# First batch of a retention and Fourier-mixing kernel: k transposed from f32, DFT sums and residual kept in PSUM, a new order

## The chip, the cores and the metric

The kernel runs on one core of a Trainium2 chip. The metric is the device time of one execution in microseconds, the median of several runs. The engines are PE (matrix products), DVE (vector), ACT (activations and copies), POOL (general) and SP, which here only starts transfers. They run side by side, each in its own order, and wait for one another through semaphores.

## The reference

Two stages follow each other. The first is linear attention with decay, for 4 batches, 8 heads, 768 positions and 64 columns per head:

```
state = gamma[h] * state + outer(k[t], v[t])
y[t]  = (1/8) * q[t] @ state
```

The heads side by side give x, 768 x 512 per batch. The second stage mixes by a Fourier transform and applies an MLP:

```
mixed = real(fft over columns (fft over positions (x)))
u     = x + mixed
un    = (u - mean(u)) / sqrt(var(u) + 1e-6)
out   = u + relu(un @ w_ch1) @ w_ch2        # 512 -> 2048 -> 512
```

Both weights and all inputs are f32 in memory; the output is 4 x 768 x 512 f32.

## The kernel before

**Attention.** Heads are treated in pairs, in the order 0, 1, 3, 2, and positions in 6 chunks of 128. For each pair q, k and v are loaded as f32 (`load_unit`, line 159), three transfers of 384 KB. POOL casts q (`q0_unit`, line 392), casts k with the decay of its position in the chunk (`k0_unit`, lines 401 to 408) and casts v (`v0_unit`, line 417), all to f16. PE transposes q and the cast k (`t0_unit`, line 433) into PSUM, six blocks each, and ACT copies them out as qT and kT (`te_unit`, lines 441 and 444). Within a chunk, PE forms scores (`am_unit`, line 458) and DVE multiplies them by a causal mask and a constant that takes the decay of k back (`ae_unit`, line 465, four instructions of 384 columns per pair). Across chunks, PE forms the products of k and v (`kv0_unit`, line 480) and DVE runs one scan over the chunks (`sc_unit`, line 489). Two groups of products, from the masked scores (`yi_unit`, line 504) and from the states (`yx_unit`, line 520), add up in PSUM, and ACT writes them, scaled, into x (`x0_unit`, line 533). x is kept in two sides: heads 0 to 3 in order, heads 4 to 7 mirrored.

**Fourier mixing.** The real transform is done by symmetry. DVE forms sums and differences of the two halves of the positions (`fold_s`, line 673), then sums and differences of the two mirrored sides (`fold_d`, line 683). PE multiplies them by cosine and sine tables over positions (`s1_unit`, line 730; four groups, each twice three products of 193 columns). ACT and DVE copy the four results into g (lines 737 and 739). Column 0 is treated apart (`g0_unit`), with a cosine table csn. The second transform (`s2_unit`, lines 843 and 847) uses tables over columns; its cosine part and sine part stand next to each other in PSUM, and their sum gives columns 0 to 256, their difference, read backwards, the rest. ACT copies the sine part to SBUF (qn, line 855) and DVE adds both, with column 0, into u (lines 856 and 858). For the first three row blocks of the first batch half of x has been added to both parts in PSUM before (`px_unit`, line 797). The mean of a row of u comes from a row sum of x (`xmean_unit`, line 711) and column 0 (`mean_unit`). The other three row blocks use g mirrored (`gr_unit`).

**MLP.** ACT writes un = mean - u (line 879), PE transposes it (`unT_unit`, line 914), ACT and DVE copy it out (lines 916 to 921). The first layer of the first three row blocks is done block by block (`h0_unit`, line 947: a row block and a quarter of the 2048 columns per unit, 16 products), all others in widths of 384 (`h_unit`, line 930). ACT and DVE evict with a relu. The second layer (`ch_unit`, line 973) gathers 16 products of 512 columns in one bank; DVE scales by the inverse deviation, adds u (line 977), and SP stores.

**Order.** The first batch is a written list (`first_units`): each unit is emitted in turn, and `pin` chains every instruction behind the one before it on its engine, so the list is the order on all engines. Where PE has nothing to do, `filler` puts products of zeros (line 145) into a bank of their own. Weights are loaded by POOL (lines 987 and 994) in eight transfers. After the first batch, the units of all batches carry due times on a scale of batches (`emit`), and a scheduler orders each engine; the next batch's loads wait for the seventh weight transfer and for one h0 product. The setup computes the sine and cosine tables on DVE and ACT (`trig_dve`, `t_act`) among the attention units.

PSUM has eight banks: five for the pool "g", two for "y" and one for the fillers; after the first batch, three of them become the MLP's pool "pm".

Of the kernel before, what the change touches and what calls it, by code (L numbers as in the profile page):

```python
# [32 lines left out]
NPE = 2  # L33
ACT_ROWS = ((2, 5, 6, 7, 8, 9, 10, 14), (0, 3, 6, 7, 9, 10, 11, 12, 14, 15), (2, 4, 5, 6, 7, 8, 10, 14))
# [3 lines left out]
def kernel(  # L38
# [32 lines left out]
    first = ExitStack()  # L71
    ps_y = first.enter_context(tc.tile_pool(name="ps_y", bufs=2, space=PSUM))
    ps_w = first.enter_context(tc.tile_pool(name="ps_w", bufs=1, space=PSUM))
    ps_pm = None
# [65 lines left out]
    wps = ps_w.tile([P, DM], f32, tag="w", name="wps")  # L140

    def filler(n):
        def run():
            for _ in range(n):
                nc.tensor.matmul(wps, wz[:, 0:P], wz, start=True, stop=True)  # L145
        return run
# [5 lines left out]
    def load_unit(b, i, after=None):  # L152
        def run():
            h0 = 2 * PAIR_ORDER[i]
            for name, src in srcs.items():
# [3 lines left out]
                dma = nc.sync.dma_start(t, src[b, h0:h0 + 2].rearrange(rows, p=P))  # L159
# [21 lines left out]
    gexp = const.tile([P, 2, H], f32, tag="gexp")  # L181
    gq8, gkd = gexp[:, 0], gexp[:, 1]
    ident16 = const.tile([P, P], f16, tag="ident16")
    tmp = up.tile([P, NCH, DM], f32, tag="u32", name="tmp")
# [3 lines left out]
    rs = [tmp[:, 2 + n] if n < 4 else tmp2[:, n - 4] for n in range(10)]  # L188
    icoln = const.tile([P, 5], f32, tag="icoln")
# [8 lines left out]
    for h in range(H):  # L198
# [6 lines left out]
                            op0=ALU.mult)  # L205
    nc.scalar.activation(gexp, gexp, AF.Exp, bias=0.0, scale=1.0)
# [4 lines left out]
    make_identity(nc, ident16)  # L211
    nc.gpsimd.affine_select(out=maskf, in_=maskf, compare_op=ALU.is_ge, fill=0.0, base=0,
# [15 lines left out]

    def late_consts():
        with tc.issue_after(lb[0]["una"].ins):  # L230
            for h in range(H):
                nc.scalar.activation(maskp[:, h // 2, h % 2], maskf, AF.Copy, bias=0.0,
                                     scale=float(gam[h] ** (-P)))
# [59 lines left out]
    def csn_unit(c):  # L293
        def run():
            nc.scalar.activation(csn[:, c, :], rs[2 * c + 1][:, 0:384], AF.Sin, bias=hpi,
                                 scale=-float(2.0 * np.pi / S))
        return run
# [46 lines left out]
    def half_ids():  # L344
        nc.gpsimd.tensor_scalar(out=hid, in0=ident16, scalar1=0.5, scalar2=1.0, op0=ALU.mult,
                                op1=ALU.mult)
        nc.gpsimd.tensor_scalar(out=nhid, in0=ident16, scalar1=-0.5, scalar2=1.0, op0=ALU.mult,
                                op1=ALU.mult)

# [3 lines left out]
    at, q16_of, kd_of, v16_of, last_cast = {}, {}, {}, {}, {}  # L353
# [42 lines left out]
    def k0_unit(i):  # L396
        def run():
            h0 = 2 * PAIR_ORDER[i]
            k32 = in_of.pop(("k", 0, i))
            kd = kd_of[0, i] = kp.tile([P, NCH, 2, D], f16, tag="kd16", name="kd16")  # L400
            nc.gpsimd.tensor_scalar(out=kd[:, :, 0, :], in0=k32[:, 0], scalar1=gkd[:, h0:h0 + 1],
                                    scalar2=1.0, op0=ALU.mult, op1=ALU.mult)
            if i < 3:
                nc.gpsimd.tensor_scalar(out=kd[:, :, 1, :], in0=k32[:, 1],
                                        scalar1=gkd[:, h0 + 1:h0 + 2], scalar2=1.0,
                                        op0=ALU.mult, op1=ALU.mult)
            else:
                nc.scalar.activation(kd[:, :, 1, :], k32[:, 1], AF.Copy, bias=0.0,
                                     scale=gkd[:, h0 + 1:h0 + 2])
        return run  # L410

    def v0_unit(i):
        def run():
            v32 = in_of.pop(("v", 0, i)).rearrange("p h c d -> p c h d")
            v16 = v16_of[0, i] = vp.tile([P, NCH, 2, D], f16, tag="v16", name="v16")
            n = NCH if i < 3 else 3
            last_cast[0, i] = nc.gpsimd.tensor_scalar(
                out=v16[:, 0:n], in0=v32[:, 0:n], scalar1=1.0, scalar2=1.0, op0=ALU.mult,
                op1=ALU.mult)
            if n < NCH:  # L420
                nc.vector.tensor_copy(v16[:, n:], v32[:, n:])
        return run

    def t0_unit(i, part):
        def run():
            if part == 0:
                at[0, i] = dict(kT=tp.tile([P, NCH, P], f16, tag="kT", name="kT"),
                                qT=qts[i % 2][:, 0])
            src = (q16_of, kd_of)[part][0, i]
            tq = at[0, i]["tq", part] = ps_g.tile([P, NCH, P], f16, tag="g", name="tq",  # L430
                                                  padded_shape=[P, 8, P])
            for c in range(NCH):
                nc.tensor.transpose(tq[:, c, :], src[:, c].rearrange("p a b -> p (a b)"), ident16)
        return run

    def te_unit(i, part):
        def run():
            st = at[0, i]
            tq = st["tq", part]
            if part == 0:  # L440
                nc.scalar.copy(st["qT"].rearrange("p c t -> p (c t)").rearrange(
# [736 lines left out]
```

## Time and profile before

| what | value |
|---|---|
| median of 3 runs | 247.5 us |
| span of the profiled execution | 246.0 us |
| PE, DVE, ACT, POOL busy | 95%, 72%, 51%, 33% |
| fillers (line 145) | 40 products, 13.3 us of PE |
| first product of the MLP (line 947) | at 35.15 us |
| second layer of the first batch (line 973) | from 48.5 us |

A row of a list of groups has the line, the engine, the operation, what it writes from what it reads, the shape and the count; then busy microseconds, the mean in nanoseconds, and the idle time ahead of it with what ended it. A row of the timeline has the start, the length, the engine, the line and the operation; in brackets the wait ahead of it. A row of a table of stretches has the stretch and its length, then the busy time and the number of instructions of each engine, the granted PE clock, the share of the DMA engines and GB/s.

### The profile page before, as it was taken

How to read it: one execution, taken by the hardware profiler on the slowest of the kernel's cores; microseconds unless marked ns; L12 is line 12 of the kernel's file. 1: busy time of each engine (PE TensorE's matmuls, PEld its weight loads, DVE VectorE, ACT ScalarE, POOL GpSimd, SP SyncE). 2: the span in 40 equal slices, each digit the busy share in tenths (PEclk: the TensorE clock that was granted, in tenths of full speed). 3: DMA queues.
4: the chain of work that ended last, by engine and by line, in shares of the span. 5: the costliest groups of instructions: out<-in, count | busy, mean ns of one | idle time of the engine just before them, and what ended most of it. 6: DMA issues, size and time to landing. Idle time of an engine off the chain costs nothing.

```text
span 246.0 us, 5309 instructions
## 1 busy us (share of the span) xinstructions
PE 234.4 (95%) x2024; PEld 144.4 (59%) x2024; DVE 177.5 (72%) x430; ACT 124.3 (51%) x276; POOL 81.3 (33%) x146
## 2 busy tenths in 40 slices
PE   6897899999999999999999999999999998999994
PEld 2454668956676655665567446665666455445543
DVE  8998957898788788995987648887895657424122
ACT  8798669477785445742247415732257217202500
POOL 6667600376500068690001637660003214000000
PEclk9999999999999999999999999999999999999999
DMA  8998999699999287988999589596100331121012
GB/s 174 257 260 138 200 204 206 152 250 261 275 233 214 56 171 176 190 174 149 242 266 210 119 183 181 108 138 150 58 0 3 60 133 30 38 85 43 0 45 85
DMA packets 99209, 36.39 MB, mean 148 GB/s; under 512 B 89840, under 2 KB 96240, under 8 KB 99184
## 3 DMA queue, kind: packets, MB, share of 16 engines
q1 hardware_dynamic: 94960, 31.86, 62.5%
q0 software_dynamic: 4224, 4.19, 10.5%
q8 instruction: 16, 0.26, 0.5%
q14 instruction: 9, 0.07, 0.1%
HBM read 27.26 MB, written 6.29 MB: 136 GB/s over the span
## 4 chain that ended last, share of the span: by engine, by line
PE 72%; DVE 8%; POOL 7%; ACT 4%; SPq 3%; DMA 2%; issue 2%; POOLq 0%; DVEq 0%
PE psc L973 30%; PE psh L930 23%; SPq L159 3%; PE ps L730 3%; PE psh L947 3%; PE wkA L594 3%; DMA k<-in_k_dram 2%; PE wkY L648 2%; POOL u L864 2%; POOL u L866 2%; PE wkY L644 1%; DVE bst L883 1%; PE wkK L613 1%; DVE u L834 1%; PE pq L827 1%
## 5 line engine op out<-in xcount | busy, mean ns | idle before, releaser
L973 PE MATMUL psc<-w,ht 128*128 128x512 f16 (+1 forms) x400 | 89.6, 370 | 0.1
L930 PE MATMUL psh<-unT,w 128*128 128x384 f16 x448 | 81.3, 326 | 0.6 <-ACT ht L934 0.6
L973 PEld LDWEIGHTS <-ht 128*128 128x128 f16 x400 | 38.1, 98 | 35.5 <-issue 0.3
L930 PEld LDWEIGHTS <-w 128*128 128x128 f16 x448 | 42.3, 98 | 24.9 <-issue 1.3
L934 ACT ACTIVATE ht<-psh 128x384 f16<-128x384 f32 x64 | 30.6, 488 | 39.4 <-PE psh L930 38.3
L864 POOL TENSOR_TENSOR u<-u,x 128x256 f32<-128x256 f32 x21 | 13.3, 634 | 102.3 <-DVE u L834 90.7
L977 DVE SCALAR_TENSOR_TENSOR ob<-psc,stats,u 128x512 f32<-128x512 f32 (+1 forms) x25 | 18.1, 722 | 27.4 <-PE psc L973 27.3
L936 DVE TENSOR_SCALAR ht<-psh 128x384 f16<-128x384 f32 x48 | 26.3, 551 | 8.6 <-PE psh L930 8.3
L597 DVE TENSOR_TENSOR atm<-wkA,maskp 128x512 f16<-128x512 f32 x36 | 23.9, 685 | 1.0 <-PE wkA L594 1.0
L885 ACT ACTIVATE un<-u,stats 128x512 f16<-128x512 f32 x21 | 15.1, 721 | 16.9 <-DVE stats L884 8.7
L883 DVE BATCH_NORM_STATS2 bst<-u 128x6 f32<-128x512 f32 x21 | 14.6, 694 | 9.7 <-POOL u L866 9.5
L623 DVE SCALAR_TENSOR_TENSOR s<-s,gk,wkK 128x128 f16<-128x128 f16 x48 | 16.4, 343 | 2.3 <-ACT s L619 1.4
L656 ACT ACTIVATE x<-wkY,gexp 128x384 f16<-128x384 f32 x24 | 12.8, 580 | 9.3 <-PE wkY L648 9.3
L145 PE MATMUL wps<-ht 128*128 128x512 f16 x40 | 13.3, 439 | 2.2 <-POOL ht L196 2.2
L377 POOL TENSOR_SCALAR kd<-k,gexp 128x384 f16<-128x384 f32 x24 | 13.8, 584 | 2.4 <-DMA k<-in_k_dram 2.4
L866 POOL TENSOR_TENSOR u<-u,x 128x256 f32<-128x256 f32 x21 | 13.3, 634 | 2.8 <-DVE u L837 1.5
L594 PE MATMUL wkA<-qTz,kT 128*128 128x256 f16 x72 | 13.6, 273 | 0.0
L829 ACT COPY qn<-pq 128x128 f32<-128x128 f32 x18 | 4.9, 274 | 14.1 <-PE pq L827 13.9
L947 PE MATMUL psh<-unT,w 128*128 128x128 f16 x192 | 11.5, 219 | 0.1
L947 PEld LDWEIGHTS <-w 128*128 128x128 f16 x192 | 11.0, 98 | 0.7 <-issue 0.5
L382 POOL TENSOR_SCALAR v<-v 128x768 f16<-128x768 f32 x12 | 10.0, 830 | 2.0 <-DMA v<-in_v_dram 1.9
L594 PEld LDWEIGHTS <-kT 128*128 128x128 f16 x72 | 6.9, 98 | 6.0 <-DVE s L623 0.4
(164 smaller groups left out, 318.2 us busy)
## 6 DMA issues: line engine op xcount, KB each, us to landing
q<-in_q_dram SPq DMA_DIRECT2D x16, 384.0 KB, 6.2
k<-in_k_dram SPq DMA_DIRECT2D x16, 384.0 KB, 5.6
v<-in_v_dram SPq DMA_DIRECT2D x16, 384.0 KB, 6.6
out_dram<-ob SPq DMA_DIRECT2D x23, 256.0 KB, 2.6
w<-in_moe_w_ch_dram POOLq DMA_DIRECT2D x8, 512.0 KB, 11.1
out_dram<-ob SPq DMA_DIRECT2D x2, 128.0 KB, 1.7
unT<-un SPq DMA_TRANSPOSE x15, 2.4
qTz<-q16z SPq DMA_TRANSPOSE x8, 3.8
```

Source lines behind the costliest of these rows:

```text
L594: mm = nc.tensor.matmul(wk[:, c2], st["kT"][:, c, :], st["qT"][:, :, c, :], start=True, stop=True)
L597: nc.vector.tensor_tensor(out=st["atm"][:, 2 * part:2 * part + 2], in0=wk, in1=maskp[:, PAIR_ORDER[i]].unsqueeze(1).to_broadcast([P, 2, 2, ...
L623: nc.vector.scalar_tensor_tensor(out=s16[:, c], in0=s16[:, c - 1], scalar=gk2[:, hp:hp + 1], in1=wk[:, c - c0], op0=ALU.mult, op1=ALU.add)
L864: nc.gpsimd.tensor_tensor(out=u[:, kb, 0:256], in0=u[:, kb, 0:256], in1=x[:, kb, 0, 1:257], op=ALU.add)
L866: nc.gpsimd.tensor_tensor(out=u[:, kb, 256:512], in0=u[:, kb, 256:512], in1=x[:, kb, 1, 257:1:-1], op=ALU.add)
L883: nc.vector.bn_stats(bst, u[:, kb, :])
L930: nc.tensor.matmul(psh, w116[:, cb, fb * P:(fb + 1) * P], unT[:, cb, rt * 384:(rt + 1) * 384], start=(cb == 0), stop=(cb == 3))
L934: nc.scalar.activation(ht16[:, fb, :], psh, AF.Relu, bias=0.0, scale=-1.0)
L936: nc.vector.tensor_scalar(out=ht16[:, fb, :], in0=psh, scalar1=-1.0, scalar2=0.0, op0=ALU.mult, op1=ALU.max)
L947: mm = nc.tensor.matmul(psh[:, f], w116[:, cb, fb * P:(fb + 1) * P], unT[:, cb, kb * P:(kb + 1) * P], start=(cb == 0), stop=(cb == 3))
L973: nc.tensor.matmul(psc[:, c0:c1], ht16[:, fb, rb3 * P:(rb3 + 1) * P], w216[:, fb, c0:c1], start=(fb == 0), stop=(fb == NFB - 1))
L977: nc.vector.scalar_tensor_tensor(out=ob[:, c0:c1], in0=psc[:, c0:c1], scalar=lb[b]["st"][:, rb, 3:4], in1=lb[b]["u"][:, rb, c0:c1], op0=AL ...
```

## The change

It rewrites the way of the first batch from the loads to the MLP. Its aims, piece by piece:

- k is loaded in halves and transposed on PE straight from f32, so that the transposes need not wait for the cast; the mask's scalar then carries the whole decay (`gks`), different for each row, in place of a constant. Transposes and evictions of k are done in halves of three chunks.
- v is cast by POOL alone. One of the 16 masks is split: ACT scales (`ac_unit`), POOL multiplies by the mask (`am2_unit`).
- `fold_d` is not used for the first batch: both sides are summed by PE, with the sine table once as it is and once negated (`nssp`, made by POOL or ACT), so each group has twice six products. Its eviction becomes a unit of its own (`ge_unit`).
- For row block 0 the residual x and both parts of the second transform are added up in PSUM, in natural order of the columns, with reversed tables (`sr_unit`); un is then written from PSUM directly, one half by ACT and one by DVE (`pn_unit`), and u later (`pu_unit`). Row blocks 1 and 2 keep the old form, in units of their own.
- csn is copied from the position cosines instead of being computed (`csn_unit`).
- The banks are divided into five "g" and three "pm" from the beginning; fillers take turns in "pm" and may be narrower than 512 columns.
- The order is a list of names, `ORDER`. It has far fewer fillers after the first pair, and eight of the twelve h0 units are in it with their evictions; four (blocks 1 and 2, quarters 0 and 2) are left to the due times. The mask constants of later batches (`late_consts`) come later. The weights' quarters are loaded in the order 2, 0, 3, 1 and 1, 2, 0, 3.

The core of the diff:

```diff
+ORDER = """
+f24_90 ts0 q0 ts2 ta02 ta00 tq0 f8_91 tka0 eq0 ts1 tkb0 eka0 f2_4 gk3 f2_10 f1_2 v0 ekb0 ta20
...
+ta30 a20 x10 f1_5 q3 kv2 a21 m200 ta32 ta40 pn2 m210 ta01 tq3 ka3 yi20 m201 x11 w12 sc2 eq3 m211
+ta31 kb3 tka3 tkb3 eka3 fsl yi21 yx2 ekb3 a30 cn0 a31 m300 v3 tL0 ac301 m311 x21 w10 kv3 m310
+x20 sL1 sc3 pm301 ta42 tL1 sr1 ta41 fs0 yx3 w13 yi31 yi30 tR0 vx31 w11 x30 sL0 g0a xm0 fs1 w21
+sR0 xm2 g0b sR1 w22 ae00 g0c ve10 tR1 af01 w20 px0 vf11 s20 w23 mean2 mean0 px2 an00 vn01 xm1
+px1 gr1 ut0 mean1 s21 xe1 au00 vu01 aq1 s22 u0 h00 aq2 u1 h02 gr3 am1 u2 h03 e00 am2 ut1 h01 e02
+vu1 e03 ut2 h13 e01 au2 h11 e13 gr2 h21 e11 h23 e21 gr0 e23
+""".split()
...
+                if b == 0 and name == "k":
...
+                    for h2 in range(2):
+                        dma = nc.sync.dma_start(t[:, :, h2], flat[:, h2])
...
+            for c3 in range(3):
+                nc.tensor.transpose(tk[:, c3, :], k32[:, 3 * half + c3].rearrange(
+                    "p a b -> p (a b)"), ident32)
...
-                scalar=float(gam[2 * PAIR_ORDER[i] + h2] ** (-P)),
+                scalar=gks[:, 2 * PAIR_ORDER[i] + h2:2 * PAIR_ORDER[i] + h2 + 1],
                 in1=maskf.unsqueeze(1).to_broadcast([P, 3, P]), op0=ALU.mult, op1=ALU.mult)
...
+                for n in range(6 if direct else 0):
+                    i0, n = 2 + P * cb, 2 * (n % 3) + n // 3
+                    if part is None or n % 2 == part:
+                        nc.tensor.matmul(ps[:, par, :],
+                                         fd[b]["ab"][:, par, n // 2, n % 2, i0:i0 + P],
+                                         tab[:, par, n // 2, :], start=par == 0 and n == 0,
+                                         stop=n == 5, skip_group_check=True)
...
+            for n in sides:
+                nc.tensor.matmul(pq[n], ident16, xts[0][:, kb, n, slice(257, 1, -1) if n else
+                                                        slice(1, 257)],
+                                 start=True, stop=False, skip_group_check=True)
...
+            else:
+                nc.scalar.activation(dst, pq[n], AF.Identity, bias=fd[0]["mu"][:, kb:kb + 1],
+                                     scale=-1.0)
...
-            for kb in range(3):
-                if kb:
-                    majors.append(unT_unit(0, kb))
-                majors += [h0_unit(kb, g) for g in range(4)]
+            majors += [lambda: None] * 8 + [h0_unit(int(x[0]), int(x[1])) for x in "22 20 12 10".split()]
...
+                streams.append(([late_consts], 0.1, 0.14))
```

In `ORDER`, tq, tka, tkb are transposes of q and of both halves of k, eq, eka, ekb their evictions, a the scores, m the masks, kv and sc the products and the scan, yi and yx the two groups of y, x or vx the evictions by ACT or DVE, fs the folds, sL, sR, tL, tR the products of the first transform (cosine and sine, left and right side), s20 to s22 the second, w the weight transfers, and f with a number the fillers in units of 128 columns.

## The prediction

> **What bounds the kernel now.** I read the page's busy shares first, then three stretches, then the order of time from the last load to the first MLP matmul.
>
> ```profile
> PE 234.4 (95%) x2024; PEld 144.4 (59%) x2024; DVE 177.5 (72%) x430; ACT 124.3 (51%) x276; POOL 81.3 (33%) x146
> ```
>
> PE is the bound on average, but the page mixes a front with fillers and a solid rest. Cut at the first MLP matmul (35.15 us) and at the first matmul of the second MLP layer (48.5 us), PE, PEld, DVE, ACT and POOL were busy for:
>
> ```profile
> 2.15:35.15 33.00, 28.79 (x326) 16.57 (x327) 29.89 (x67) 26.16 (x56) 19.66 (x35) 1.00 1.17 218
> 35.15:48.50 13.35, 13.10 (x212) 12.27 (x212) 9.23 (x23) 9.98 (x28) 2.71 (x8) 1.00 0.96 177
> 48.50:246.00 197.50, 192.48 (x1491) 115.53 (x1488) 137.15 (x328) 86.83 (x192) 57.51 (x94) 1.00 0.66 136
> ```
>
> From 35.15 us PE hardly waits. Before it, 13.31 us of PE's time are the idle-time fillers of line 145:
>
> ```profile
> 0.00:35.15 35.15, 13.31 (x40) 3.72 (x40) 1.00 1.10 206
> ```
>
> So only the moment matters at which the MLP of the first batch starts; each microsecond won there should reach the end. DVE leads that front (29.89 of 33.00), ACT is next. The timeline from the last k load:
>
> ```profile
> 21.47 1.29 POOL L401 TENSOR_SCALAR kd<-k,gexp 128x384 f16<-128x384 f32 x1
> ...
> 22.81 0.51 PE L433 MATMUL tq<-ident,kd 128*128 128x128 f16 x6 [0.73 <-POOL kd L401]
> ...
> 23.36 0.80 ACT L444 COPY kT<-tq 128x768 f16<-128x768 f16 x1 [0.92 <-PE tq L433]
> ```
>
> and on to the first MLP matmul:
>
> ```profile
> 24.62 1.02 DVE L465 SCALAR_TENSOR_TENSOR atm<-wkA,maskf 128x384 f16<-128x384 f32 x2 [0.92 <-PE wkA L458]
> ...
> 27.27 1.05 ACT L533 ACTIVATE x<-wkY,gexp 128x384 f16<-128x384 f32 x2 [0.70 <-PE wkY L504]
> ...
> 28.81 0.62 DVE L673 TENSOR_TENSOR xab<-x 128x384 f16<-128x384 f16 x2
> 29.46 1.03 DVE L683 TENSOR_TENSOR eo<-xab 128x768 f16<-128x768 f16 x2
> 31.32 0.59 DVE L739 CAST g<-ps 128x386 f16<-128x386 f32 x1 [0.32 <-PE ps L730]
> 32.29 0.37 ACT L855 COPY qn<-pq 128x255 f32<-128x255 f32 x1 [0.83 <-PE pq L847]
> 33.44 0.91 ACT L879 ACTIVATE un<-u,mu 128x256 f16<-128x256 f32 x2
> 34.72 0.37 ACT L916 COPY unT<-pst 128x256 f16<-128x256 f16 x1 [0.38 <-PE pst L914]
> 35.15 3.00 PE L947 MATMUL psh<-unT,w 128*128 128x128 f16 x48
> ```
>
> The reader is to see one chain: cast, transpose, eviction, scores, mask, then folds, first DFT, second DFT, u, un, unT.
>
> **What the Trainium skill says.** (1) "FP8 and Floating Point Precision", TensorE Precision Notes: a true f32 product takes four passes of the array; but "TensorE: Matmul & The Clock Gate", Terms, says that trn2's transpose mode is 4 times faster for f32. No f32 transpose is in the trace, so its cost is open between one and four passes. (2) "TensorE: Matmul & The Clock Gate", Part 1: the array starts at half clock and falls back after an idle window of about 3.4 us. The trace agrees with the start: the first six fillers take 2.74 us, three at 7.84 us take 0.81. No fall back is seen. (3) "ScalarE: Activation LUTs", What ACT_TABLE_LOAD costs: 186 + 0.833 N ns for an activation with immediates; for 384 columns 506, and line 934 measures 488.
>
> **The change part by part.**
>
> Loads. Each k load of the first batch becomes two halves, with the same bytes and 256 B rows. The queue is full until about 20.7 us anyway. Worth nothing; k of the last pair still lands at 21.3 us (issue at 14.47 plus 6.8 to landing), v at 22.6.
>
> k from f32. The last pair's chain from k to scores was 21.3 to 24.25. Now six f32 transposes, two evictions and two score groups in halves. One transpose: 0.055 us (one pass, as the f16 ones at 0.51 for six with their drain) to 0.45 (four passes, loads not hidden); I take 0.22, four passes with loads hidden. Transposes end at 21.35 + 6 x 0.22 = 22.7. The PE order then has a yi group and a yx group (0.35 + 0.5) before the scores, so these run at 23.6 to 24.2, and the first mask at about 24.1 instead of 24.62: 0.5 us. It is the wait for ACT that can eat it, see below. POOL's decay cast leaves this chain.
>
> DVE. To the end of the last fold sum (29.43 before) the new order removes the first half of the differences (1.03), the v cast (0.54, now on POOL) and one mask of 16 (0.49, to ACT and POOL); it adds a third decay row (0.14, the spacing of lines 202 and 204) and one x eviction (0.55, as line 936 for 384 from PSUM). Net -1.37: 29.43 becomes 28.06 if DVE's waits stay as they are. The other half of the differences (1.03) behind it is gone too; the DFT reads the sums directly.
>
> ACT. In the new order I add ACT from 6.05 us to the last x eviction: 4 q evictions of 0.80 (3.2), 8 half k evictions of 0.49 (3.9), 13 table activations of 0.41 to 0.66 (6.8), 4 scan constants of 0.40 (1.6), 7 x evictions of 0.54 (3.8), 3 cosine copies at 0.45, between lines 225 and 934 (1.35), 2 reversed sines of 0.41 (0.8) and the one mask scaling (0.49): 21.95, so 28.0 with no wait at all. Before, the same stretch had 18.57 of 22.5 busy. I allow 0.3 us of waits and get 28.3. ACT then sets the last fold sum: 28.3 + 0.62 = 28.9. The ends of this step are 28.1 (DVE alone) and 30 (1.7 us of waits).
>
> DFT. All four groups take 12 instead of 6 matmuls of 193 columns: 24 more at 0.094 (18 in 1.69 on the chain of waits) = 2.3 us of PE. Three quarters lie ahead of the last fold sum, where fillers were. Behind it remain 9: 0.85 + 0.2 of drain, so 30.1. Evictions 0.6: 30.7, against 31.9.
>
> Residual in PSUM. The second DFT's tail is four matmuls of 256 columns, 0.11 each: with drain 31.3. Then un is read from PSUM on ACT and DVE at once, 0.5. Gone from the chain: qn 0.37, u 0.97 (two of 0.48) and the second un. But on ACT the order puts one row sum (0.65 + 0.2, measured 0.73 with overlap) between un and the first half of unT, so ACT is at un 31.35 to 31.85, row sum to 32.6, unT to 32.95. First MLP matmul at 33.0 against 35.15: **2.15 us earlier**. The u additions, queued on DVE behind unT, wait for nobody but the un of the next row blocks.
>
> From there to the second layer the work is that of before: 192 matmuls, two transpositions, three mirrored DFT rows, 13.35 us; four of its evictions move to ACT, the mask constants behind them. ACT has 9.98 of 13.35 and DVE 9.23, so no new wait. Second layer at 46.35.
>
> Limits behind it. The seventh weight transfer lands at 26.9 + 15.8 = 42.7 us and the eighth at 45.0; the new order needs the seventh first. POOL issues them in a similar place (the first after the first half of k, the second after v at 22.6 + 0.83). 46.35 is later than 42.7, and the eighth is needed 2.6 us after the start. The next batch's loads, issued at 44.97, can come at 43.0 at the earliest, 2 us earlier, about as much as PE. So 2.2 us survive.
>
> **The rivals.**
>
> A, forecast: 2.2 us, 247.5 - 2.2 = 245.3.
>
> B, more: ACT and DVE run without waits, fold sum at 28.1 to 28.3, the f32 transpose costs one pass (-1 us on the last pair), the first matmul comes at 31.5: 3.6 us, 243.9. Beyond it stands the weight landing: 48.5 - 42.7 = 5.8 us at most, 241.7. For: DVE's removed work is certain. Against: ACT's sum leaves no room.
>
> C, nothing: 0.45 us per f32 transpose makes 2.7 us for the last pair, 1.4 more than I took, and ACT's evictions wait with it; with the earlier pairs also late 2 us are lost: 247.3. For: the f32 operands hold PE 10.8 us in all, and PE is in order. Against: PE had 13.3 us of fillers to give.
>
> D, slower: the fillers after the first pair are almost gone, PE falls to half clock while it waits for loads, and its own 15 us of real work ahead of 35 us cost 3 to 6 us more; or an in-order queue stands behind a wait that the new order placed badly. 250 to 253, say 251.5. For: ACT's queue mixes three pairs, and one late half holds all behind it. Against: transposes of the next pair fill many of the holes.
>
> **How the numbers follow.** A 0.45, B 0.23, C 0.20, D 0.12. Predicted 245.3. The range runs from 242.0, nearly the limit of B, to 249.5, which takes in C and the mild part of D. Faster by over 2% is below 242.55: the outer part of B, 0.12. Slower by over 2% is above 252.45: half of D, 0.07. The rest, 0.81, is within 2%.
>
> **What would show it.** Right: the first MLP matmul near 33 us and the second layer near 46.3; ACT busy without holes from 6 to 32 us and the last x eviction ending at 28 to 29; f32 transposes near 0.22 us apart; no difference lines left for the first batch; loads of the next batch at 43 to 43.5; PE's waits after the second layer's start still about 5 us. Wrong: 512-column fillers or DFT matmuls at half rate after 10 us (D); a transposing pitch of 0.1 or 0.45; the mask of the last pair later than 24.6 us; PE waiting for weights at 42 to 45 us (the limit of B); or a changed late order that gives the gain back in PE's waits behind 50 us.

## The result and the profile after

The changed kernel took 250.31 us (median of four runs, 248.87 to 250.66), the kernel before 247.49 beside it (median of four, one of which took 843 us): a ratio of 1.0104, 95% interval 1.0073 to 1.0134. It is 1% slower, by about 2.8 us, where the forecast had it 2.2 us faster. In the profiled executions the span grew from 246.0 to 248.8 us. First the page's busy line of the changed kernel, then the same three stretches as before the change, cut at its own first MLP matmul (34.12) and at its own second layer (46.84), then the fillers (line 154) of the first stretch:

```profile
PE 232.1 (93%) x2027; PEld 147.4 (59%) x2027; DVE 178.7 (72%) x428; ACT 123.0 (49%) x277; POOL 84.3 (34%) x150
```

```profile
2.15:34.12 31.97, 26.51 (x329) 19.71 (x330) 29.02 (x68) 25.89 (x61) 22.72 (x43) 0.95 1.14 213
34.12:46.84 12.72, 12.66 (x215) 12.33 (x213) 9.97 (x24) 7.74 (x22) 1.57 (x3) 1.00 1.13 192
46.84:248.80 201.96, 192.95 (x1489) 115.38 (x1486) 138.39 (x330) 88.07 (x195) 58.61 (x96) 1.00 0.64 134
```

```profile
0.00:34.12 34.12, 5.32 (x17) 1.80 (x17) 0.95 1.07 201
```

The front is 1.03 us shorter (34.12 against 35.15) and the stretch behind it another 0.63. But the last stretch, whose code was not touched, is 201.96 instead of 197.50 us long for the same 193 us of PE's work: 4.5 us lost, mostly in PE's idle time, which went from 5.0 to 9.0. In the front the PE clock is 0.95, and DVE is again busy nearly throughout. The timeline of the changed kernel from the last pair's transposes of k to the first MLP matmul:

```profile
22.39 0.97 PE L487 MATMUL tk<-ident,k 128*128 128x128 f32 x6
...
23.73 0.86 ACT L496 CAST kT<-tk 128x384 f16<-128x384 f32 x2
...
24.97 1.67 DVE L517 SCALAR_TENSOR_TENSOR atm<-wkA,gexp,maskf 128x384 f16<-128x384 f32 x3
...
28.44 0.58 ACT L607 ACTIVATE x<-wkY,gexp 128x384 f16<-128x384 f32 x1 [0.91 <-PE wkY L574]
...
29.13 0.62 DVE L749 TENSOR_TENSOR xab<-x 128x384 f16<-128x384 f16 x2
...
31.23 0.60 DVE L805 CAST g<-ps 128x386 f16<-128x386 f32 x1 [0.17 <-PE ps L829]
...
32.32 0.47 ACT L964 ACTIVATE un<-pq,mu 128x256 f16<-128x256 f32 x1 [0.98 <-PE pq L944]
...
33.32 0.37 ACT L1115 COPY unT<-pst 128x256 f16<-128x256 f16 x1
...
34.12 0.39 PE L1143 MATMUL psh<-unT,w 128*128 128x128 f16 x4
```

The last fold sum ends at 29.75, later than before (29.43). All that the front won was won behind it: 4.37 us from there to the MLP instead of 5.72. The last wait of PE over 0.1 us ahead of the MLP ends at 24.05, with a mask of DVE; in the stretches behind it PE is full:

```profile
24.05 0.26 PE L574 MATMUL wkY<-v,atm 128*128 128x64 f16 x3 [0.60 <-DVE atm L517]
```

```profile
24.00:29.75 5.75, 5.61 (x93) 4.89 (x94) 5.29 (x13) 4.81 (x13) 4.22 (x7) 1.00 1.06 168
29.75:34.12 4.37, 4.37 (x55) 3.95 (x53) 2.88 (x13) 3.31 (x11) 1.50 (x4) 1.00 1.23 201
```

So DVE sets the front up to 24.05, and from there PE's own list does; the last x eviction and un wait for PE (0.91 and 0.98 us above).

Where did the end go? PE's waits behind 46 us in the changed kernel (of whom, total, times, longest) have two rows at the top that the kernel before does not have at all:

```profile
PE wkA L669 <- DMA kT<-kd: 2.7, 2, 1.6
...
PEld L669 <- DMA kT<-kd: 3.6, 2, 1.9
```

From the third batch on, k is transposed by DMA; line 669 (594 before) needs the result for the scores. PE's timeline around it, before:

```profile
106.60 0.38 PE L594 MATMUL wkA<-qTz,kT 128*128 128x256 f16 x2
...
112.93 0.38 PE L594 MATMUL wkA<-qTz,kT 128*128 128x256 f16 x2
```

and after:

```profile
107.67 0.39 PE L669 MATMUL wkA<-qTz,kT 128*128 128x256 f16 x2 [1.56 <-DMA kT<-kd]
...
115.33 0.39 PE L669 MATMUL wkA<-qTz,kT 128*128 128x256 f16 x2 [1.16 <-DMA kT<-kd]
```

SP issues loads, stores and transposes in one order. Its queue over that time, before:

```profile
87.78 0.79 SPq L159 DMA_DIRECT2D q<-in_q_dram  x1
92.22 0.36 SPq L981 DMA_DIRECT2D out_dram<-ob  x1
93.17 1.52 SPq L542 DMA_TRANSPOSE qTz<-q16z  x1
94.80 1.55 SPq L544 DMA_TRANSPOSE kT<-kd  x1
...
97.50 0.83 SPq L159 DMA_DIRECT2D v<-in_v_dram  x1
98.91 3.23 SPq L542 DMA_TRANSPOSE qTz<-q16z  x1
102.25 1.94 SPq L544 DMA_TRANSPOSE kT<-kd  x1
```

and after:

```profile
91.57 0.36 SPq L1182 DMA_DIRECT2D out_dram<-ob  x1
92.52 1.55 SPq L617 DMA_TRANSPOSE qTz<-q16z  x1
94.17 1.54 SPq L619 DMA_TRANSPOSE kT<-kd  x1
95.78 0.57 SPq L187 DMA_DIRECT2D q<-in_q_dram  x1
...
98.00 2.95 SPq L187 DMA_DIRECT2D v<-in_v_dram  x1
101.13 3.63 SPq L617 DMA_TRANSPOSE qTz<-q16z  x1
104.88 1.21 SPq L619 DMA_TRANSPOSE kT<-kd  x1
```

One line has moved: the load of q of the last pair of the third batch stood ahead of a store and of the first pair's transposes, and stands behind them now. The second pair's k transpose is issued 2.6 us later. The moved load holds SP for only 0.57 us; most of the rest is the load of v behind it, which now takes 2.95 us instead of 0.83, and why it does isn't shown. The scheduler moved the load by itself, with the late code the same, because the front it plans from is another.

The loss can be followed in the starts of DVE's last additions (ob). The lead of the changed kernel is 0.66 us at the end of the first batch's MLP (85.42 against 86.08), then -1.08 (114.21 against 113.13) behind the first wait, -2.41 (119.94 against 117.53) behind the second, -2.21 at the last one. The rest of the 2.8 is at the very end. Before and after:

```profile
242.86 0.48 DVE L977 SCALAR_TENSOR_TENSOR ob<-psc,stats,u 128x256 f32<-128x256 f32 x1 [1.26 <-PE psc L973]
```

```profile
245.07 0.48 DVE L1178 SCALAR_TENSOR_TENSOR ob<-psc,stats,u 128x256 f32<-128x256 f32 x1 [1.26 <-PE psc L1174]
```

From there to the end of the span it is 3.14 us before and 3.7 after.

### The profile page after: what moved, and what is told of

It reads as the page before. It is cut to its first block, busy times and chain, and to the rows that moved or that the text cites. A ratio compares the mean times of both kernels' runs of the same rounds, so it can differ in the third digit from the quotient of the medians.

```text
span 248.8 us, 5329 instructions
## 1 busy us (share of the span) xinstructions
PE 232.1 (93%) x2027; PEld 147.4 (59%) x2027; DVE 178.7 (72%) x428; ACT 123.0 (49%) x277; POOL 84.3 (34%) x150
## 4 chain that ended last, share of the span: by engine, by line
PE 46%; POOL 5%; DMA 3%; DVE 2%; issue 1%; ACT 1%; SPq 0%; POOLq 0%
PE psc L1174 24%; PE psh L1124 16%; DMA kT<-kd 2%; PE ps L835 2%; PE wkA L669 1%; POOL kd L409 1%; DMA qTz<-q16z 1%; POOL v L414 1%; PE wkY L723 1%; POOL u L1053 1%; POOL q16z L406 1%; PE pq L1025 1%; POOL u L1055 1%; PE wkY L719 1%; DVE u L1032 1%
## 5 line engine op out<-in xcount | busy, mean ns | idle before, releaser
L672 DVE TENSOR_TENSOR atm<-wkA,maskp 128x512 f16<-128x512 f32 x36 | 24.1, 685 | 3.4 <-PE wkA L669 3.4
L1032 DVE SCALAR_TENSOR_TENSOR u<-pq,g,qn 128x256 f32<-128x256 f32 x18 | 8.5, 471 | 1.7 <-ACT qn L1028 1.5
```

The costliest lines, as they stand in the source:

```text
L672: nc.vector.tensor_tensor(out=st["atm"][:, 2 * part:2 * part + 2], in0=wk, in1=maskp[:, PAIR_ORDER[i]].unsqueeze(1).to_broadcast([P, 2, 2, ...
```

## The experiments

All ratios are to the kernel before on the same chip (247.5 us beside the change, 247.7 to 247.8 beside the others), with 95% intervals. "Lead" is by how much a run's moment comes earlier than in the first profile of before: at the first MLP matmul (35.15), at the last addition of the first batch's MLP but two (86.08), and at the last addition of all (242.86). A ratio is from all runs, a lead from one profile, and the two need not go together: mask_const's profile is one of its slower runs (247.31, median 246.57), that of qf_w its fastest (247.24, median 247.68). mask_const leaves out the rows' decay; all others compute the whole.

| run | ratio | lead: MLP | at 86 | last |
|---|---|---|---|---|
| the change | 1.0104 (1.0073 to 1.0134) | 1.03 | 0.66 | -2.21 |
| q_ahead | 1.0026 (1.0016 to 1.0036) | 0.74 | 0.37 | 0.36 |
| q_behind | 1.0032 (1.0020 to 1.0044) | 0.07 | 0.08 | -0.84 |
| fill | 1.0133 (1.0119 to 1.0146) | 1.04 | 0.69 | -2.45 |
| fill_q_ahead | 1.0077 (1.0060 to 1.0094) | 1.40 | 1.02 | -1.13 |
| q_first | 1.0000 (0.9992 to 1.0008) | 0.62 | 0.27 | 0.51 |
| qf_w | 0.9996 (0.9985 to 1.0006) | 1.30 | 0.94 | 1.16 |
| w_nomm | 0.9997 (0.9989 to 1.0005) | 0.92 | 0.56 | 0.79 |
| mask_const | 0.9959 (0.9947 to 0.9971) | 1.66 | 0.84 | 1.03 |
| v_decay | 0.9999 (0.9983 to 1.0015) | 1.96 | 1.05 | 1.24 |
| best | 1.0007 (0.9997 to 1.0017) | 0.85 | 0.69 | 0.93 |
| best_fill | 1.0039 (1.0024 to 1.0054) | 0.85 | 0.70 | 0.06 |
| lanes | 0.9999 (0.9991 to 1.0008) | 0.50 | 0.14 | 0.37 |
| k_split_2 | 1.0009 (1.0000 to 1.0019) | 0.45 | 0.45 | 0.45 |
| late_v_2 | 1.0005 (0.9995 to 1.0015) | 1.14 | 0.77 | 0.99 |
| vd_late_2 | 0.9997 (0.9981 to 1.0013) | 1.94 | 0.78 | 1.00 |
| vd_late_fill_2 | 0.9984 (0.9973 to 0.9995) | 1.30 | 1.05 | 1.10 |

**The place of one load.** q_ahead puts the load of q ahead of the first transposes again (still behind the store):

```diff
-    streams.append(([load_unit(b + 1, i) for i in range(4)], b + -0.370, b + 0.075))
+    streams.append(([load_unit(b + 1, i) for i in range(3)], b + -0.370, b + -0.03625))
+    streams.append(([load_unit(b + 1, 3, None, "q")], b + -0.025, b + -0.025))
+    streams.append(([load_unit(b + 1, 3, None, "kv")], b + 0.075, b + 0.075))
```

> The changed kernel with one transfer put back in its old place on the SP queue: the load of q of the last pair of the third batch stands again ahead of the first two DMA transposes, not behind them; the order on every other engine is as in the changed kernel. Theory (the late SP order ate the gain): the two waits of PE for k's DMA transposes at 107.7 and 115.3 us go, which is about 3 us, so 247.3 us, between 246.5 and 247.8; the first MLP matmul stays at 34.1. Rival (the loss is in the front, half clock of PE, and the two waits would come from something else, such as the lead shrinking): 249.5 to 250.5, with the waits for k's transposes still there.

q_behind is the reverse in the kernel before: its load of q is chained behind the first k transpose of the third batch.

> The kernel before with that same load of q moved behind the first two DMA transposes, which is the late order of the changed kernel without its front. Theory: PE waits for k's DMA transposes of the third batch and the time grows by about 3 us, to 250.5 (249.5 to 251.5). Rival (the late order is harmless without the new front): 247.3 to 247.8.

q_first puts the load ahead of the store too, by chaining the store behind it, and gives the queue its old late order whole.

> The changed kernel with the load of q of the last pair of the third batch put ahead of the output store as well, so that the SP queue's late order is that of the kernel before to the last instruction; all other engines as in the changed kernel. Theory now (two causes: the queue's order, and the loads of the second batch, which start only 0.56 us earlier than before and so let only some 0.6 us of the lead through): no wait of PE for k's transposes, the second k transpose issued at 101.5 to 102.5 instead of 103.6 with the load behind the store, and an end 0.3 to 0.7 us ahead of before (ratio 0.997 to 0.999). Rival (the transposes' moment is fixed by something else, casts or the DMA engines): as with the load behind the store, ratio 1.002 to 1.003.

Measured: in q_ahead and q_first PE, DVE, ACT and POOL have the lists of the changed kernel, instruction by instruction, and SP's differs by this one load. No matmul of PE waits longer than 0.1 us for k's transposes any more, and the ratio falls from 1.0104 to 1.0026 and to 1.0000. The queue of q_first:

```profile
87.51 0.78 SPq L187 DMA_DIRECT2D q<-in_q_dram  x1
91.95 0.36 SPq L1183 DMA_DIRECT2D out_dram<-ob  x1
...
98.64 4.41 SPq L618 DMA_TRANSPOSE qTz<-q16z  x1
103.18 1.22 SPq L620 DMA_TRANSPOSE kT<-kd  x1
```

So the place of this load is the cause of the loss: undone, all of the 1% is gone. The rival, that the loss is in the front, falls. The sizes were not all met. q_ahead was forecast at 247.3 us and took 248.3. The k transpose of q_first comes at 103.18 and not at 101.5 to 102.5, and the end is no better than before. q_behind cost 0.8 us, not 3: in the kernel before, the same place of the load makes only the first of the two waits (0.74 us), not the second.

The second wait needs one thing more. The third k transpose of the batch, issued at 110.36, landed 4.9 us later in the changed kernel, but after 3.1 us in before (issued at 108.44), q_ahead, q_first and q_behind. After 3.1 us it would have been there at 113.5, ahead of PE, which came to it at about 114.2. The lists of DMA queues while it was on its way (queue, packets, MB, share of 16 engines), for the change (110.36 to 115.28) and for q_first (108.67 to 111.76):

```profile
q1 hardware_dynamic: 2680, 0.66, 87.9%
q8 instruction: 1, 0.02, 1.4%
```

```profile
q1 hardware_dynamic: 2282, 0.57, 100.3%
```

In the change one transfer of 16 KB, of the queue that the profile names "instruction", starts at 113.1, ahead of the landing. In before, q_first, q_ahead and q_behind it starts at 112.07, 112.29, 112.78 and 113.81, each time 0.5 to 0.6 us behind the landing. So the moved load, by issuing the third transpose later, seems also to have laid it across this transfer. The profiles of all 18 kernels bear this out: of their 144 k transposes by DMA 36 took 3.8 us or more, and each of these had such a transfer under way before it landed; of the other 108, none above 3.5 us, 13 had. That is read from traces, and no run moved this transfer by itself, so that it is not shown as a cause.

**PE's clock.** fill adds six products of zeros where PE stood idle from 13.0 to 14.8 us; fill_q_ahead has q_ahead's edit too.

```diff
-... eka1 yi00 a11 ...
+... eka1 f24_91 yi00 a11 ...
```

> The changed kernel with six more filler matmuls of 512 columns on PE, ahead of the first product with masked differences, where PE stood idle from 13.0 to 14.8 us; the late order unchanged. Rival theory (the halved PE clock from 16 to 20 us set the front back): clock 1.0 from 16 to 20, DVE's chain and the first MLP matmul about 1 us earlier, at 33.1, and the end about 1 us earlier or, if the late waits absorb it, the same. Main theory: DVE is the bound of the front, so the first MLP matmul moves by less than 0.4 us, and the late waits leave 250.0 to 250.4.

> Both edits at once: the load of q back ahead of the transposes and the six fillers. Main theory: as with the load alone, 247.3, at most 0.4 us less. Rival (clock matters): 246.3 or less, the first MLP matmul at about 33.1.

Two stretches of the changed kernel, 10 to 15 and 15 to 20 us (the clock is the third number from the end):

```profile
10.00:15.00 5.00, 2.51 (x35) 1.83 (x35) 4.86 (x11) 4.83 (x12) 4.93 (x9) 1.00 1.27 251
15.00:20.00 5.00, 4.94 (x76) 3.79 (x74) 4.93 (x10) 3.49 (x8) 4.09 (x7) 0.66 1.26 252
```

and of fill_q_ahead:

```profile
10.00:15.00 5.00, 3.93 (x43) 2.45 (x43) 4.86 (x11) 4.85 (x12) 4.82 (x9) 1.00 1.27 250
15.00:20.00 5.00, 4.06 (x75) 2.88 (x72) 4.93 (x10) 3.73 (x9) 4.21 (x7) 1.00 1.26 253
```

A mean of 0.66 over 5 us is 3.4 us at half clock. q_first, with 0.73 and 0.58 in these stretches, has twice as much. The first MLP matmul comes at 33.75 without such a spell (fill_q_ahead), at 34.12 with one (the change) and at 34.41 and 34.53 with two (q_ahead, q_first): some 0.3 to 0.4 us each. For the change that is about a third of what its front lacks (1.03 instead of 2.15), and no part of the loss behind: DVE is busy 4.86 and 4.93 of 5 us with and without it. fill itself still had one spell, a little earlier, and its front did not move.

The surprise is that fill_q_ahead, with the earliest front of these four, is slower than q_ahead by 0.5%. PE waits again:

```profile
106.36 0.39 PE L669 MATMUL wkA<-qTz,kT 128*128 128x256 f16 x2 [0.62 <-DMA kT<-kd]
...
113.84 0.39 PE L669 MATMUL wkA<-qTz,kT 128*128 128x256 f16 x2 [0.98 <-DMA kT<-kd]
```

The second k transpose was issued at 103.56, as in q_ahead (103.64), though PE came 0.66 us earlier. Its first transposes still had the lead (92.20 against 92.85), the load of k behind them no longer (98.12 against 98.02); what held the queue between isn't shown. The wait near 114 costs more than the lead itself: the third k transpose, issued at 109.04, landed 4.8 us later. Here too the instruction transfer starts ahead of the landing, at 111.39, while in q_ahead it came at 112.78. fill, which has the same fillers, has it at 112.52, and its third k transpose took 4.7 us.

**The loads of the second batch.** qf_w is q_first with the weight transfers w10, w13, w11 and w21 earlier in `ORDER`, ahead of v's last cast and of POOL's product with the mask. w_nomm has the same in the changed kernel, and its loads of the second batch no longer wait for a product of the first layer; this also puts q and k of the third batch's last pair ahead of the first transposes.

```diff
-                    for x in (w_dma[after].ins, lb[0]["mm"].ins):
+                    for x in (w_dma[after].ins,):
```

> The same, and four of the eight weight loads moved ahead of a cast and of the masked product on POOL (no other engine changes). Theory: weights land 1 to 2 us earlier, but the loads of the second batch also wait for a matmul of the first layer on PE, at about 44.4, so they start at most 0.4 us earlier and the end gains at most 0.4 us on the kernel without this edit. Rival (weights alone were the gate): loads at 42.5 and an end 1.5 us earlier.

> The changed kernel with four weight loads earlier on POOL and the loads of the second batch no longer waiting for the matmul of the first layer, only for the seventh weight load (this also moves q and k of the last pair of the third batch ahead of the first transposes, and leaves v alone behind them). Theory (the loads of the second batch are the floor that the lead fell on): loads from about 42.5, 1.9 us earlier; the lead over before at the end of the first batch's MLP grows from 0.66 to about 1.7; end about 1.5 us ahead of before (ratio 0.994), if the third batch's transposes follow. Rival (DVE's work of the second batch is the floor): the lead there stays at 0.7 and the ratio at 0.998 or above.

The loads began at 44.15 and 44.10 against 44.41 in the changed kernel, so neither kernel had the loads at 42.5. In qf_w the seventh weight transfer landed at 42.75, 1.0 us earlier than in q_first (43.77), and SP then waited 1.3 us for the product of the first layer, as expected; that wait was 2.3 us in before, 1.0 in q_first and 0.4 in the change. w_nomm doesn't wait for it, but its seventh transfer, issued at 27.99 instead of 29.54, landed at 44.05 and not earlier than in the change (43.91). late_v_2 further below has w_nomm's loads with the old order of weights, and its loads began at 43.55. The lead at 86 us is 0.36 less than at the MLP in qf_w and w_nomm, as in the change (0.37), q_ahead (0.37), q_first (0.35) and late_v_2 (0.37). So these 0.4 us are lost with loads at 43.55 as at 44.83 (q_first); PE waits there for DVE (0.93 us idle from 46.84 to 85.42 in the change, 0.22 in the same stretch before), in an order of products that the scheduler also changed. The theory that the loads pass on only 0.6 us of lead is wrong for leads up to 1.4. With the leads of 1.66 to 1.96 further below (mask_const, v_decay, vd_late_2) 0.8 to 1.2 us are lost by 86 us, with new waits of PE for POOL's casts of the second batch, which wait for the loads of k; there the loads do bite.

**The pointer in the masks.** mask_const is q_first with a constant as the masks' scalar. v_decay keeps the result whole in another way: rows' decay on v, constants on k. Of v_decay's edit:

```diff
-            nc.vector.scalar_tensor_tensor(
+            nc.vector.tensor_tensor(
                 out=st["atm"][:, 3 * half:3 * half + 3, h2, :], in0=st["wk", half][h2],
-                scalar=gks[:, 2 * PAIR_ORDER[i] + h2:2 * PAIR_ORDER[i] + h2 + 1],
-                in1=maskf.unsqueeze(1).to_broadcast([P, 3, P]), op0=ALU.mult, op1=ALU.mult)
+                in1=maskf.unsqueeze(1).to_broadcast([P, 3, P]), op=ALU.mult)
...
-                out=v16, in0=in_of["v", 0, i].rearrange("p h c d -> p c h d"), scalar1=1.0,
...
+                    out=v16[:, :, h2, :], in0=in_of["v", 0, i][:, h2], scalar1=gks[:, h:h + 1],
```

> The kernel with the load ahead of the store, with a constant in place of the per-partition pointer in the 15 masked differences on DVE (leaves out the rows' decay of the first batch). Theory: each 0.55 us instead of 0.60, so about 0.8 us less of DVE ahead of the spectrum, and the first MLP matmul at 33.3 to 33.6 instead of 34.1; the loads of the second batch still wait for weights, so the end moves by less than 0.3 us. Rival (the pointer costs nothing on the path): first MLP matmul within 0.2 us of the kernel with the pointer.

> The kernel with the load of q ahead of the store, with the rows' decay of the first batch put on v in its cast (two POOL instructions of 0.58 us with a pointer, in place of one of 0.83) instead of on the masked differences, which become plain products on DVE; k's cast takes a constant. Theory (the pointer in the mask is what the front lost on DVE): each mask about 0.55 us, first MLP matmul at 33.4 to 33.8 against 34.1 to 34.5, ratio to before 0.995 to 0.998. Rival (POOL, nearly full from 10 to 20 us, becomes the bound with 0.35 us more in each pair): first MLP matmul no earlier than 34.1, ratio 1.000 or above.

Groups of the first 34 us (count, busy us, mean ns), the change, mask_const and v_decay:

```profile
L517 DVE SCALAR_TENSOR_TENSOR atm<-wkA,gexp,maskf 128x384 f16<-128x384 f32 x15 | 8.5, 603 | 0.5 <-PE wkA L510 0.5
```

```profile
L518 DVE SCALAR_TENSOR_TENSOR atm<-wkA,maskf 128x384 f16<-128x384 f32 x15 | 7.6, 542 | 0.5 <-PE wkA L511 0.5
```

```profile
L520 DVE TENSOR_TENSOR atm<-wkA,maskf 128x384 f16<-128x384 f32 x15 | 7.6, 546 | 1.1 <-PE wkA L513 1.1
```

The pointer costs 60 ns in each of 15 masks, 0.9 us of a saturated DVE, and the first MLP matmul follows: 33.49 and 33.19 against 34.53. From the end of PE's last wait of more than 0.2 us (24.47 in q_first, 23.32 in mask_const, 22.96 in v_decay) to the first MLP matmul it is 10.06, 10.17 and 10.23 us, so DVE's queue sets the front up to that wait and PE's list the rest. mask_const's end moved by 0.4%, more than the "less than 0.3 us" expected, so leads do reach the end. But v_decay, with the earliest front of all, has a median of 247.50 and runs from 246.8 to 249.66: the mean gains nothing. Of its lead of 1.96 us 0.9 is gone by 86 us, with waits of PE for kd, which POOL casts (0.6 us of products and 1.1 us of weight loads).

best (v_decay with qf_w's weight order) and best_fill (four fillers more, in the place of fill's six) were meant to add up.

> The same with four weight loads earlier on POOL. Theory: weights do not land earlier (the first kernel with that edit started the second batch's loads at 44.15, without it 44.4 to 44.8), so within 0.2 us of the kernel without this edit. Rival (with an earlier front the weights and the loads behind them hold the lead): 0.4 us or more ahead of it.

> The same with four more filler matmuls of 512 columns on PE ahead of the first product with masked differences. Theory: no spell of half clock in most runs (clock 1.0 instead of 0.98 to 0.99), worth about 0.35 us for each spell of 3.4 us; ratio 0.001 to 0.002 lower than without. Rival: the fillers push the front as much as the clock gains, no difference.

They did not: with v's longer casts (1.60 us together, 0.82 in qf_w) and the weights' transfers both ahead of it, POOL's product with the mask came late, PE waited 1.15 us for it at 28.07, and the first MLP matmul was at 34.30 in both. best_fill then had PE wait 0.7 us for the third k transpose (at 113.08) in spite of the old queue order: it landed 4.6 us after its issue, in best 3.1, with the same lead of 0.7 at 86 us. The two programs differ in four fillers of PE and in nothing else, and the instruction transfer starts at 111.02 in best_fill, ahead of the landing (113.03), and at 112.34 in best, behind it (111.65). So four fillers at 13 us cost a wait at 113; that they did it by shifting this transfer fits the traces but is not tested apart.

**The end of the program.** lanes is q_first with four late stores in halves, so that eight transfers are added to those of before and not four; k_split_2 is the kernel before with only the first batch's loads of k in halves, by this edit:

```diff
-                dma = nc.sync.dma_start(t, src[b, h0:h0 + 2].rearrange(rows, p=P))
+                flat = src[b, h0:h0 + 2].rearrange(rows, p=P)
+                if b == 0 and name == "k":
+                    for h2 in range(2):
+                        dma = nc.sync.dma_start(t[:, h2], flat[:, h2])
+                else:
+                    dma = nc.sync.dma_start(t, flat)
```

> The kernel with the load of q ahead of the store, with four output stores late in the third and early in the fourth batch each split into halves of 256 columns, so that the number of transfers differs from the kernel before by eight instead of four. Theory (the end of the program, 3.65 us from the start of the last addition against 3.14 before, is longer by the waits of SP for its transfers' semaphores that come after the last store's in turn): about 0.3 us shorter end, 3.4 or less. Rival: the length of the end has nothing to do with it, 3.6 to 3.7.

> The kernel before with k's four loads of the first batch each split in halves, as the changed kernel has them, and nothing else. Theory (the four more transfers make the end of the program longer): from the start of the last addition to the end of the span 3.4 to 3.7 us instead of 3.14; time 0.3 to 0.6 us above before. Rival (the end is longer for another reason): 3.14 and no difference in time.

From the last addition to the end: 3.53 us in lanes and 3.38 in k_split_2 (last addition at 242.41, span 245.8), against 3.14 in before and 3.68 in q_first. lanes thus won half of the 0.3 us forecast. At the end SP waits for nine semaphores of its transfers in turn, 0.06 us each when they are set. In the trace of before, in q_behind and in lanes the one that is set last stands ninth; in k_split_2, q_first and the change it stands fifth, and four more follow, 0.25 us. So four more transfers cost 0.25 us at the end: k_split_2, which has nothing else, shows it. The other 0.3 us are in one late step of POOL, 0.37 to 0.39 us in the change, q_first and lanes and 0.08 in before, q_behind and k_split_2. Why is open. The ratio of k_split_2 is no worse than 1.0009 because halves of k also bring the front forward, by 0.45 in its one profile, which the forecast had put at nothing. Its median is that of before (247.75); five of its 20 runs lie at 248.5 to 249.0, and without their traces the reason is open.

**More slack for the transposes.** late_v_2 is the changed kernel with w_nomm's edit of the loads, q and k of the last pair ahead of the first transposes and v chained behind the second pair's; vd_late_2 adds v_decay's edit, vd_late_fill_2 four fillers.

```diff
+                    streams.append(([load_unit(2, 3, None, "qk")], b + 0.075, b + 0.075))
+                    streams.append(([load_unit(2, 3, None, "v")], b + 0.12, b + 0.12))
```

> The changed kernel with its front as it is; in the third batch the loads of q and k of the last pair ahead of the first transposes, and its load of v behind the second pair's, so that no load stands between the two pairs of transposes (the second batch's loads also no longer wait for the matmul of the first layer). Theory (slack of k's second transposes): the second k transpose is issued at 100 to 101.5, no wait of PE for it in any run; ratio to before 0.999 to 1.000, 1.0 % below the changed kernel. Rival (v comes too late now): PE waits for v or for k's transpose of the last pair near 115 to 120, ratio above 1.002.

> The same late order with the rows' decay on v instead of on the masks. Theory: first MLP matmul at 33.2 as in the run with the decay on v, about 1.2 us of lead at the last addition in every run, ratio 0.996 to 0.998, no run above 247.9. Rival (another wait takes the lead): ratio 0.999 or above.

> The same with four more fillers ahead of the first product with masked differences. Theory: a clock of 1.0 in more runs, ratio 0.0005 to 0.0015 below the kernel without them. Rival: no difference or slower.

The queue of late_v_2:

```profile
97.27 1.92 SPq L622 DMA_TRANSPOSE qTz<-q16z  x1
99.30 1.24 SPq L624 DMA_TRANSPOSE kT<-kd  x1
100.59 0.58 SPq L187 DMA_DIRECT2D v<-in_v_dram  x1
```

The k transpose is issued 5.6 us earlier than in the change, no profile of the three has a wait for it, and the 1% is gone again (1.0005). No wait took its place, but the extra slack gave nothing beyond q_first either. vd_late_fill_2 is the only version that computes everything and is measurably faster than before, by 0.16% (0.05 to 0.27); that is 0.4 us out of a lead of 1.10 at the last addition, the rest is the longer end. vd_late_2 had runs at 248.85 and 248.95, and vd_late_fill_2 one at 248.84, against the expectation (of 59 runs of the kernel before, one was above 248.1), so something still takes the lead in some executions; without their traces it stays open.

## Why the prediction was wrong

The step that failed is "From 35.15 us PE hardly waits" with what it was taken to mean, "each microsecond won there should reach the end", and the conclusion "So 2.2 us survive". It took PE's late stretch as a block of work that moves as a whole. PE hardly waited there because the transposes by DMA came just in time: the second k transpose of the third batch, issued at 102.25 and landing 3.8 us later, was there 0.5 us before PE used it at 106.60. A lead on PE alone, or a later transpose, turns this into a wait. The change did both, PE being 0.5 us earlier there and the transpose 2.6 us later by one load moved in SP's queue; that made PE wait 1.56 us, and 1.16 us for the third transpose, which took 4.9 us to land instead of 3.1, with the instruction transfer under way. The sentence at the end of the prediction, "a changed late order that gives the gain back in PE's waits behind 50 us", names what happened, but no time was worked out for it. Rival D comes nearest: 250.31 lies in its 250 to 253, and it speaks of "an in-order queue" behind "a wait that the new order placed badly". But its reason was ACT's queue in the front and its 3 to 6 us were half clock, so that its number met is luck. The moved load could have been seen: the order of SP's queue is fixed with the program.

Point by point:

- **Front, 2.15 us.** Half in size: 1.03 us. Behind the last fold sum the sum held, 4.37 us against 4.1 forecast. Ahead of it the forecast had 0.5 us of gain and the run lost 0.3. "Net -1.37" for DVE left out the pointer in the masks (15 times 60 ns, 0.9 us), which mask_const and v_decay give back, and half-clock spells cost 0.3 to 0.4 each. With the pointer gone and one such spell (v_decay) the front was at 33.19, close to the 33.0 forecast. But it ran on PE's list and not, as forecast, on ACT's.
- **f32 transposes, 0.22 us each.** Too high. Six take 0.97 with a last one of 0.27, so they follow each other at 0.14. The Trainium skill, "TensorE: Matmul & The Clock Gate", Terms, has the transpose mode 4 times faster for f32; but 0.14 lies midway between the prediction's one pass (0.055; in before the f16 transposes follow each other at 0.06) and four (0.22), and the weight load of such a block took 0.14 too, 0.10 in f16, so the trace does not confirm one pass. The last pair's transposes began at 22.39, not 21.35: PE's list has them behind products that wait for DVE's masks. The last pair's masks came at 24.97, not at 24.1, later than before (24.62), so that faster transposes, on which rival B counted, won nothing here.
- **ACT.** "28.3" for the last x eviction: measured 29.02, with a wait of 0.91 for PE. "ACT then sets the last fold sum" is the part that failed: PE set it, by products that ran without a wait from 24.05, when a mask of DVE released them. Three quarters of the 24 additional products of the first transform were counted as free, where fillers had stood; behind 24.05 no such room was left.
- **Residual in PSUM, DFT sums on PE.** As forecast: un at 32.32 against 31.35, 0.97 late as the fold sum was 0.85 late.
- **Loads of the next batch at 43.0 to 43.5.** 44.41: the seventh weight transfer landed at 43.91 instead of 42.7, and the product of the first layer, which the loads also wait for, came 0.4 us behind it.
- **Second layer at 46.35.** 46.84, since the front was 1.1 us late. The stretch of 13.35 became 12.72 with the same 192 products of the first layer in it; PE's busy time in it fell from 13.10 to 12.66 and its idle time from 0.25 to 0.06. Why the same products took less isn't shown.
- **Rival D, half clock.** It came, for one or two spells of 3.4 us, at 0.3 to 0.4 us each instead of the 3 to 6 us worked out, while DVE was the bound. The Trainium skill, "TensorE: Matmul & The Clock Gate", Part 1, has the clock halved after at least one idle window of a free-running 3413 ns. The trace agrees with the length of the spell (3.4); but an idle stretch of 1.8 us (13.0 to 14.8), in 5 us of which PE was busy 2.51, was enough here. Part 4 (PE-mode transpose) adds that transposes don't count as PE busy in the same way; six stand right ahead of the gap, from 12.13, which would make it 2.7 us. No run tried that apart.
- **Loads of k in halves, "worth nothing".** 0.45 us of front by themselves, 0.25 us lost at the end.

## What to carry to other kernels

When one stage of a scheduled kernel is rewritten, compare the order of every engine and above all of the DMA queue in the stages that were not touched: one moved load can cost more than the stage won. "PE hardly waits" says how things are, not how much slack there is; look for the landing next ahead of PE's use and take the difference (here 0.5 us) before counting a gain as one that reaches the end. Where a DMA transpose lands late, look into the list of DMA queues for a transfer of another queue, instructions included: here its time shifted with the number of fillers in PE's list. On a saturated DVE count also the operand forms, since 60 ns on each of 15 instructions were nearly half of what the front was to win.

## What the runs showed of the hardware

- A masked product of 384 columns from PSUM took 603 ns with a per-partition pointer as its scalar and 542 with a constant; a plain product took 546.
- PE's granted clock was half for 3.4 us within 15 to 20 us of the change, behind an idle stretch of 1.8 us (13.0 to 14.8), and for twice that in q_ahead and q_first.
- An f32 transpose of 128 x 128 followed the one ahead of it at 0.14 us in the change, one in f16 at 0.06 in before.
- Of 144 k transposes by DMA in 18 profiles 108 landed 2.7 to 3.4 us after their issue began and 36 after 3.8 to 4.9. In each of the 36 a 16 KB transfer of the queue "q8 instruction" was under way before the landing, in 13 of the 108 too. With four more fillers in PE's list this transfer came 1.3 us earlier (best_fill, 111.02 against 112.34).
- Four transfers more in a program, whose last store's semaphore then stands fifth and not ninth among those that SP waits for: 0.25 us.
